# Head 0 of an attention and gated-product kernel: loads and splits in smaller pieces on two queues, the last maxima ranked later, 28 filler products in place of 72

## The chip, the cores and the metric

The kernel runs on one core of a Trainium2 chip. The metric is the device time of one execution in microseconds (us). The core has four compute engines: TensorE (PE in the profile; its weight loads are PEld), VectorE (DVE), ScalarE (ACT) and GpSimd (POOL). SyncE (SP) and ScalarE also issue the DMA transfers.

## The reference

Attention over 4 batches and 8 heads, with q pooled over pairs of rows, and then a gated product over the result:

```python
q_pool = q.reshape(B, H, S // 2, 2, D).mean(axis=3)      # 576 rows a head, D = 64
scores = scale * np.matmul(q_pool, k.transpose(0, 1, 3, 2))   # 576 x 1152
scores = scores - np.max(scores, axis=-1, keepdims=True)
attn = np.exp(scores); attn = attn / (np.sum(attn, axis=-1, keepdims=True) + 1e-09)
x = np.matmul(attn, v)                                   # then (2304, 512)
gate = 1.0 / (1.0 + np.exp(-(x @ w_gate)))               # d_ff = 1536
return (gate * (x @ w_val)) @ w_out
```

## The kernel before

**A head.** There are 32 heads (`u` = 0 to 31). Each fp32 operand is split into a part that TensorE's fp32r format holds and the rest of it. `q_sum` adds the two pooled rows, `q_hi` (ScalarE) rounds, `q_lo` subtracts for the rest; `k_hi` and `k_lo` do the same for K. Then come the *maxima*: for each tile `t` of 128 query rows (five tiles, the last of 64 rows) three products of 384 keys (`mm`, L412 for head 0, L504 for the others), each followed by a row maximum on VectorE (`rmax`, L417 and L510). `all_max` (L329) joins three maxima, and `diags` (L335, L338) writes them as diagonal blocks beside q, so that a score comes out with its maximum already taken off. Only then can the *scores* run (L610: two products for 288 queries by 128 keys, 18 such scores a head in two halves), then the exponentials on ScalarE (L614), then the products with V (L628 in the first batch, 36 instructions a head). The first half (`GR[0]`, queries 0 to 287) waits for the diagonals of tiles 0 to 2 (`got`), the second half for those of tiles 3 and 4 as well (`got1`).

**Head 0** has its own function, `first_head`. Its transfers are cut in pieces (`QS`, `KS`) and its maxima in two groups of tiles (`TS`). Head 1 and the later ones go through `head_operands`: `q_sum` L455 and `q_lo` L465 on GpSimd, `q_hi` L460 and `k_hi` L475 on ScalarE, `k_lo` L481 on GpSimd, `diags` L335 and L338 on GpSimd. The raw q and K lie in one buffer each (`qr`, `kr`). So head 1's q can be loaded (L442) only when head 0's `q_hi`, `q_hi2` and `q_lo` have read `qr`, and head 1's K (L439) only when head 0's `k_hi` and `k_lo` have read `kr`.

**The order.** Nothing runs in the order in which it stands. Every operation goes into a plan, `pl.op(engine, duration, function, priority, after=..., late=...)`. The planner walks through time with these assumed durations: whenever an engine is free, it takes the ready operation with the lowest priority number (an engine other than PE may also hold back for up to `WAIT` = 0.4 us for a more urgent one). `late` is the assumed delay of a transfer after its issue, `behind` puts an issue behind another one. Then 30 rounds of a random search shift some priorities by up to 1 and keep what ends earlier in the plan. The result is one fixed sequence for each engine; on the chip, each engine runs its own sequence in order, and waits at an instruction whose operands are not there.

**The fillers.** `busy` (L951) issues products of a constant tile `sel` with itself into a bank that nothing reads. Before, there are 18 operations of four such products, with priorities from -5.

Of the kernel before, what the change touches and what calls it, by code (L numbers as in the profile page):

```python
# [13 lines left out]
ACTF = mybir.ActivationFunctionType  # L14
ALU = mybir.AluOpType
# [176 lines left out]
def attention_glu_kernel(ctx: ExitStack, tc: tile.TileContext, qT, kT, vt_in, v, wg, wv, wo, out):  # L192
    nc = tc.nc
    B, H, D = 4, 8, 64
    SK, SQ = 1152, 576
# [13 lines left out]
    pl = Plan(SLOTS, ("b",))  # L209
# [6 lines left out]
    late = ctx.enter_context(ExitStack())  # L216
# [96 lines left out]
    AHEAD = 50  # L313
    BUSY = 18
    KEEP = 0.15
    LAST_GATE = 215
    QLP = lambda u: 1 <= u < 2 * H
# [6 lines left out]
    LO, HI, ALL = slice(0, 64), slice(64, 128), slice(0, 128)  # L324


    def all_max(o, ts):
        for p, a, b in ((ALL, ts[0], min(ts[-1] + 1, 4)),) + (((LO, 4, 5),) if 4 in ts else ()):
            nc.vector.tensor_reduce(out=o[p, a:b, 3], in_=o[p, a:b, 0:3], axis=AXX, op=ALU.max, negate=True)  # L329

    def diags(eng, o, q, ts):
        a, b = ts[0], min(ts[-1] + 1, 4)
        q2 = q[1][LO, 128 * a:128 * b].rearrange("p (a c) -> p a c", c=64)
        for par, p in enumerate((LO, HI)):
            eng.tensor_tensor(out=q2[:, par:2 * (b - a):2], in0=ident[p, p].unsqueeze(1).to_broadcast([64, b - a, 64]),  # L335
                              in1=o[p, a:b, 3].unsqueeze(2).to_broadcast([64, b - a, 64]), op=ALU.mult)
        if 4 in ts:
            eng.tensor_tensor(out=q[1][LO, 512:SQ], in0=ident[LO, LO], in1=o[LO, 4, 3:4].to_broadcast([64, 64]), op=ALU.mult)  # L338

    def first_head():  # L340
        kh, qh, kr, qr, pm, vr = (pl.hold(x) for x in ("K", "Q", "kr", "qr", "pm", "ve"))
        QS, KS, TS = ((0, 384), (384, SQ)), ((0, SQ), (SQ, SK)), ((0, 1, 2), (3, 4))
        lq, lk = [], []
        for k, (a, b) in enumerate(QS):

            def load_q(a=a, b=b):
                nc.sync.dma_start(out=tl(qr)[:, :, a:b], in_=qT[0][:, :, a:b])

# [12 lines left out]
        def load_v():
            nc.sync.dma_start(out=tl(vr)[:, :, 0], in_=v[0])

        lv = pl.op("SP", dma(288), load_v, -50, take=[vr], late=3.0)
        lks, qh_done, max_in, kb = (lk[:2], lk[2:]), [], [], []
        for k, (a, b) in enumerate(QS):

            def q_sum(a=a, b=b):
                r = tl(qr)
                nc.vector.tensor_tensor(out=r[:, 0, a:b], in0=r[:, 0, a:b], in1=r[:, 1, a:b], op=ALU.add)  # L370

            def q_hi(a=a, b=b):
                nc.scalar.activation(out=tl(qh)[0][LO, a:b], in_=tl(qr)[:, 0, a:b], func=ACTF.Copy)

            def q_lo(a=a, b=b):
                qa = tl(qh)[0]
                eng = nc.gpsimd if a else nc.vector
                eng.tensor_tensor(out=qa[HI, a:b], in0=tl(qr)[:, 0, a:b], in1=qa[LO, a:b].bitcast(F32),
                                  op=ALU.subtract)

            o = pl.op("DVE", dve(b - a), q_sum, -40 + 4 * k, after=[lq[k]], uses=[qr])
            o = pl.op("ACT", act(b - a), q_hi, -40 + 4 * k, after=[o], uses=[qr] + ([qh] if k else []), take=[] if k else [qh])
            qh_done.append(o)
            max_in.append(pl.op("POOL" if k else "DVE", 0.6 if k else 0.5, q_lo, -40 + 4 * k, after=[o], uses=[qr, qh]))
        ka = []
        for k, (a, b) in enumerate(KS):

            def k_hi(a=a, b=b):
                nc.scalar.activation(out=tl(kh)[0][:, a:b], in_=tl(kr)[:, a:b], func=ACTF.Copy)

            def k_lo(a=a, b=b):
                nc.gpsimd.tensor_tensor(out=tl(kh)[1][HI, a:b], in0=tl(kr)[HI, a:b], in1=tl(kh)[0][HI, a:b].bitcast(F32),
                                        op=ALU.subtract)

            o = pl.op("ACT", act(SQ), k_hi, -39 + 2 * k, after=lks[k], uses=[kr] + ([kh] if k else []),
                      take=[] if k else [kh])
            ka.append(o)
            kb.append(pl.op("POOL", pool(SQ), k_lo, -12 + k, after=[o, max_in[1]], uses=[kr, kh]))

        def q_hi2():  # L400
            nc.scalar.activation(out=tl(qh)[1][HI, 0:SQ], in_=tl(qr)[:, 0], func=ACTF.Copy)

        qb = pl.op("ACT", act(SQ), q_hi2, -35, after=qh_done, uses=[qr, qh])
        dg = []
        for k, ts in enumerate(TS):
            red = []
            for t in ts:
                for j in range(3):
                    m = pl.hold("b")

                    def mm(t=t, j=j, m=m):
                        nc.tensor.matmul(out=tl(m)[LO if t == 4 else ALL, 0:384], lhsT=tl(qh)[0][:, t * 128:min(SQ, t * 128 + 128)],  # L412
                                         rhs=tl(kh)[0][:, j * 384:(j + 1) * 384], start=True, stop=True)

                    def rmax(t=t, j=j, m=m):
                        p = LO if t == 4 else ALL
                        nc.vector.tensor_reduce(out=tl(pm)[p, t, j:j + 1], in_=tl(m)[p, 0:384], axis=AXX, op=ALU.max)  # L417

                    new = not (k or red)
                    a = pl.op("PE", pe(384), mm, -21 + 3 * t + j, after=[max_in[k]] + ([ka[0]] if j == 0 else ka),  # L420
                              uses=[qh, kh], take=[m])
                    red.append(pl.op("DVE", 0.49, rmax, -21 + 3 * t + j, after=[a], uses=[m] + ([] if new else [pm]),
                                     take=[pm] if new else [], keep=KEEP))

            o = pl.op("DVE", 0.1, lambda ts=ts: all_max(tl(pm), ts), -21 + 3 * ts[-1] + 2.5, after=red, uses=[pm])
            dg.append(pl.op("DVE", 1.0 if len(ts) > 2 else 0.7, lambda ts=ts: diags(nc.vector, tl(pm), tl(qh), ts),
                            -21 + 3 * ts[-1] + 2.6, after=[o], uses=[pm, qh]))
        return dict(k=kh, q=qh, v=vr, lv=lv, got=[dg[0], qb] + max_in + ka + kb, dg1=[dg[1]], hi_k=ka, hi_q=qh_done + [qb])

    def head_operands(u, need):  # L430
        if u == 0:
            return first_head()
# [524 lines left out]
    xs, x_done = {}, {}
    blocked = [pl.hold(tag) for tag, n in LATE.items() for _ in range(n)]
# [79 lines left out]
```

## Time and profile before

| | us |
|---|---|
| median of 3 timed runs | 920.72 (920.59 to 921.58) |
| span of the profiled execution, first to last instruction | 919.1 |
| median less that span | 1.6 |
| PE busy in the profile | 910.0 |
| head 0's first filler, first maximum product, first score | 2.73, 9.58, 16.65 |

The profile comes from one execution. A group's busy time over its count is the time of one instruction. The products on PE overlap, so that the distance between starts is what one more product costs. The granted clock stands at 1.00 in all 40 slices of the span.

### The profile page before, as it was taken

The page shows a single profiled execution, that of the slowest core. Times are in us where ns is not written, and L with a number is a line of the kernel's source. Part 1 is how long each engine was busy: PE and PEld are TensorE (multiplying, and loading weights), DVE is VectorE, ACT ScalarE, POOL GpSimd, SP SyncE. Part 2 cuts the span into 40 slices and gives each one's busy share as a digit, 9 for nine tenths or more (in the row PEclk, how much of TensorE's full clock was granted, in tenths as well). Part 3 has the DMA queues.
Part 4 walks back from the last instruction along what each step waited for, and adds up shares of the span by engine and source line. Part 5 has one row for each costly group of instructions (what it writes and reads, how often), then busy time and mean ns, then how long its engine had stood idle before and what let it go on. Part 6 is the DMA issues. An engine that isn't in the chain of part 4 may idle for free.

```text
span 919.1 us, 18605 instructions
## 1 busy us (share of the span) xinstructions
PE 910.0 (99%) x6371; PEld 882.8 (96%) x6371; DVE 649.5 (71%) x1427; ACT 657.5 (72%) x1703; POOL 671.1 (73%) x669
## 2 busy tenths in 40 slices
PE   8999999999999999999999999999999999999998
PEld 8888888999999999999999999999999999999998
DVE  6677779888898987878787878877777874510112
ACT  4798899989998886777887677677877767422111
POOL 6765366889888989889899888888889877521211
PEclk9999999999999999999999999999999999999999
DMA  6899888788868666555644455554545423435432
GB/s 140 212 289 247 275 254 261 239 266 273 262 210 275 206 202 192 161 157 149 166 136 142 131 157 157 160 148 132 166 123 158 142 93 115 166 139 183 162 115 75
DMA packets 57616, 166.27 MB, mean 181 GB/s; under 512 B 17393, under 2 KB 21745, under 8 KB 51377
## 3 DMA queue, kind: packets, MB, share of 16 engines
q1 hardware_dynamic: 57360, 164.78, 59.3%
q8 instruction: 50, 0.82, 0.4%
q10 hardware_dynamic: 160, 0.30, 0.1%
q14 instruction: 46, 0.37, 0.1%
HBM read 132.12 MB, written 23.59 MB: 169 GB/s over the span
## 4 chain that ended last, share of the span: by engine, by line
PE 91%; ACT 4%; DVE 3%; POOL 1%; DMA 1%; issue 1%; POOLq 0%; ACTq 0%; DVEq 0%
PE bank L846 47%; PE bank L610 15%; PE bank L504 7%; PE bank L628 7%; PE bank L657 6%; PE bank L653 6%; PE bank L730 1%; DVE pm L417 1%; PE bank L951 1%; DMA wg<-wg_d 1%; ACT eh L614 1%; ACT bank L643 0%; ACT KA L475 0%; DMA wo<-wo_d 0%; DVE el L646 0%
## 5 line engine op out<-in xcount | busy, mean ns | idle before, releaser
L846 PE MATMUL bank<-x,wg 128*128 128x288 f32 x2304 | 353.8, 295 | 0.0
L846 PEld LDWEIGHTS bank<-x,wg 128*128 128x128 f32 x2304 | 325.6, 188 | 1.1 <-ACT sg L889 0.4
L646 DVE TENSOR_TENSOR el<-bank,eh 128x288 fp32r<-128x288 f32 x432 | 192.9, 452 | 70.7 <-ACT bank L643 65.9
L510 DVE TENSOR_REDUCE pm<-bank 128x1 f32<-128x384 f32 (+1 forms) x375 | 199.7, 550 | 49.6 <-PE bank L504 45.0
L614 ACT ACTIVATE eh<-bank 128x288 fp32r<-128x288 f32 x432 | 176.4, 409 | 73.1 <-PE bank L610 65.9
L643 ACT ACTIVATE bank<-bank 128x288 f32<-128x288 f32 x432 | 176.9, 410 | 0.2
L610 PE MATMUL bank<-QA,KA 128*128 128x288 f32 x576 | 175.1, 308 | 1.5 <-DVE pm L510 0.9
L610 PE MATMUL bank<-QB,KB 128*128 128x288 f32 x576 | 167.4, 295 | 0.0
L903 POOL TENSOR_TENSOR g<-sg,g 128x288 fp32r<-128x288 f32 x96 | 79.9, 833 | 105.2 <-ACT g L899 102.7
L675 POOL TENSOR_TENSOR acc<-acc,eh 128x576 f32<-128x576 f32 x92 | 132.5, 1440 | 16.7 <-ACT eh L614 14.6
L846 PE MATMUL bank<-g,wo 128*128 128x288 f32 x864 | 139.2, 295 | 0.2
L657 PE MATMUL bank<-el,vt 128*128 128x288 f32 x432 | 127.2, 296 | 0.5 <-DVE el L646 0.5
L653 PE MATMUL bank<-eh,vt 128*128 128x288 f32 x432 | 127.3, 296 | 0.0
L846 PEld LDWEIGHTS bank<-g,wo 128*128 128x128 f32 x864 | 125.0, 188 | 1.2 <-DMA wo<-wo_d 0.3
L504 PE MATMUL bank<-KA,QA 128*128 128x384 f32 (+1 forms) x375 | 125.7, 350 | 0.2
L610 PEld LDWEIGHTS bank<-QA,KA 128*128 128x128 f32 x576 | 108.2, 188 | 5.9 <-DVE pm L510 1.3
L610 PEld LDWEIGHTS bank<-QB,KB 128*128 128x128 f32 x576 | 108.3, 188 | 1.3
L895 DVE SCALAR_TENSOR_TENSOR sg<-sg,bank 128x288 f32<-128x288 f32 x96 | 43.3, 451 | 81.2 <-PE bank L846 79.2
L657 PEld LDWEIGHTS bank<-el,vt 128*128 128x128 f32 x432 | 81.1, 188 | 1.5 <-DVE el L646 1.2
L653 PEld LDWEIGHTS bank<-eh,vt 128*128 128x128 f32 x432 | 81.1, 188 | 0.7 <-ACT eh L614 0.3
L675 POOL TENSOR_TENSOR acc<-eh,eh 128x576 f32<-128x576 f32 x48 | 68.7, 1431 | 15.6 <-ACT eh L614 10.9
L628 PE MATMUL bank<-e,ve 128*128 128x288 f32 x288 | 76.6, 407 | 0.0
(86 smaller groups left out, 1359.6 us busy)
## 6 DMA issues: line engine op xcount, KB each, us to landing
wg<-wg_d SPq DMA_DIRECT2D x48, 1024.0 KB, 5.2
wo<-wo_d SPq DMA_DIRECT2D x36, 512.0 KB, 3.9
kr<-in_kT_dram SPq DMA_DIRECT2D x62, 288.0 KB, 5.0
wg_d<-cs SPq DMA_DIRECT2D x24, 512.0 KB, 5.0
qr<-in_qT_dram SPq DMA_DIRECT2D x31, 288.0 KB, 4.1
KP<-KA SPq DMA_DIRECT2D x30, 288.0 KB, 4.4
vr<-in_v_dram SPq DMA_DIRECT2D x24, 288.0 KB, 3.1
cr<-in_wg_dram SPq DMA_DIRECT2D x12, 512.0 KB, 5.3
```

Source lines behind the costliest of these rows:

```text
L504: nc.tensor.matmul(out=tl(m)[LO if t == 4 else ALL, 0:384], lhsT=lhs(t), rhs=rhs()[:, j * 384:(j + 1) * 384], start=True, stop=True)
L510: nc.vector.tensor_reduce(out=o, in_=tl(m)[p, 0:384], axis=AXX, op=ALU.max)
L610: nc.tensor.matmul(out=tl(m)[:, 0:GN], lhsT=tl(hd["k"])[k][:, ks], rhs=tl(hd["q"])[k][:, a:b], start=(k == 0), stop=(k == 1))
L614: nc.scalar.activation(out=ev(), in_=tl(m)[:, 0:GN], func=ACTF.Exp, scale=1.0 / 16.0)
L628: nc.tensor.matmul(out=tl(av[0])[:, 0:GN], lhsT=pair(c, 0), rhs=tl(h), start=(c == 0), stop=(c == NC - 1))
L643: nc.scalar.activation(out=p, in_=p, func=ACTF.Exp, scale=1.0 / 16.0)
L646: nc.vector.tensor_tensor(out=tl(el), in0=tl(m)[:, 0:GN], in1=ev().bitcast(F32), op=ALU.subtract)
L653: nc.tensor.matmul(out=tl(av[0])[:, 0:GN], lhsT=pair(c, w), rhs=ev(), start=(c == 0), stop=(c == NC - 1))
L657: nc.tensor.matmul(out=tl(av[1])[:, 0:GN], lhsT=pair(c, 1 - w), rhs=tl(el), start=(c == 0), stop=(c == NC - 1 and not mine_c))
L675: nc.gpsimd.tensor_tensor(out=tl(acc), in0=tl(old).bitcast(F32), in1=tl(eh).bitcast(F32), op=ALU.add)
L846: nc.tensor.matmul(out=ps[:, 0:GN], lhsT=l, rhs=r, start=(n == 0 and j == 0), stop=(n == 3 and j == 2))
L903: nc.gpsimd.tensor_tensor(out=g[:, 1, a:b], in0=tl(sg), in1=g[:, 0, a:b].bitcast(F32), op=ALU.subtract)
```

## The change

It touches head 0 and the fillers, and nothing else in the text of the kernel; the order of everything is planned anew.

- q is loaded in three pieces (128, 256 and 192 columns) and K in three (384 each, two halves of 64 partitions), where there were two of each. The second piece of q goes on ScalarE's queue, as the first of K does already.
- The first two pieces of q are summed and split on VectorE; the third is summed and split on GpSimd, with low priorities. `k_lo` has three pieces. `q_hi2` has two.
- A maximum product waits only for the pieces that it reads. The maxima, `all_max` and `diags` of tiles 3 and 4 get priorities from -1 on, where they had -12 on. The first half of the scores no longer waits for the third piece of q.
- The fillers are 14 operations of two products, with priority 999.

```diff
-    BUSY = 18
+    BUSY = 14
...
-        QS, KS, TS = ((0, 384), (384, SQ)), ((0, SQ), (SQ, SK)), ((0, 1, 2), (3, 4))
+        QS, KS, TS = ((0, 128), (128, 384), (384, SQ)), ((0, 384), (384, 768), (768, SK)), ((0, 1, 2), (3, 4))
...
+            def load_q(a=a, b=b, eng=nc.scalar if k == 1 else nc.sync):
+                eng.dma_start(out=tl(qr)[:, :, a:b], in_=qT[0][:, :, a:b])
+
+            lq.append(pl.op("ACT" if k == 1 else "SP", 0.6, load_q, (-60, -55, -53)[k], uses=[qr] if k else [], take=[] if k else [qr], late=(1.7, 2.2, 3.4)[k],
...
+                lk.append(pl.op("SP" if k else "ACT", 0.6, load_k, (-59, -57, -57)[k], uses=[] if new else [kr],
+                                take=[kr] if new else [], late=(2.0, 2.2, 3.0)[k], behind=lk[0] if k == 1 and not n else lk[-1] if lk else None))
...
-        lks, qh_done, max_in, kb = (lk[:2], lk[2:]), [], [], []
+        lks, qh_done, max_in, kb = (lk[:2], lk[2:4], lk[4:]), [], [], []
...
+                (nc.gpsimd if a > 128 else nc.vector).tensor_tensor(out=r[:, 0, a:b], in0=r[:, 0, a:b], in1=r[:, 1, a:b], op=ALU.add)
...
+            o = pl.op("POOL" if a > 128 else "DVE", pool(b - a) if a > 128 else dve(b - a), q_sum, (-40, -36, -18.5)[k], after=[lq[k]], uses=[qr])
...
+            max_in.append(pl.op("POOL" if a > 128 else "DVE", pool(b - a) if a > 128 else dve(b - a), q_lo, (-40, -36, -11)[k], after=[o], uses=[qr, qh]))
...
-            kb.append(pl.op("POOL", pool(SQ), k_lo, -12 + k, after=[o, max_in[1]], uses=[kr, kh]))
...
+            kb.append(pl.op("POOL", pool(b - a), k_lo, -20 + k, after=[o, max_in[1]], uses=[kr, kh]))
...
+            qb.append(pl.op("ACT", act(b - a), q_hi2, -30 if a else -35, after=qh_done[2 * (a > 0):2 + (a > 0)], uses=[qr, qh]))
...
-                    a = pl.op("PE", pe(384), mm, -21 + 3 * t + j, after=[max_in[k]] + ([ka[0]] if j == 0 else ka),
...
+                    a = pl.op("PE", pe(384), mm, (-10 if k else -21) + 3 * t + j, after=[max_in[2 if k else min(t, 1)]] + ka[:j + 1],
...
-        return dict(k=kh, q=qh, v=vr, lv=lv, got=[dg[0], qb] + max_in + ka + kb, dg1=[dg[1]], hi_k=ka, hi_q=qh_done + [qb])
+                            (-10 if k else -21) + 3 * ts[-1] + 2.6, after=[o], uses=[pm, qh]))
+        return dict(k=kh, q=qh, v=vr, lv=lv, got=[dg[0], qb[0]] + max_in[:2] + ka + kb, dg1=[dg[1], qb[1], max_in[2]], hi_k=ka, hi_q=qh_done + qb)
...
-            for _ in range(4):
+            for _ in range(2):
...
-            pl.op("PE", 0.7 if k < 6 else 0.36, busy, -5 + 0.01 * k, uses=[bz] if k else [], take=[] if k else [bz])
+            pl.op("PE", 1.5 if k == 0 else 0.44, busy, 999 + 0.01 * k, uses=[bz] if k else [], take=[] if k else [bz])
```

## Rows read from the trace of the kernel before

**Rows 1.** The page's 40 slices: TensorE's busy share and granted clock, in tenths.

```profile
PE   8999999999999999999999999999999999999998
...
PEclk9999999999999999999999999999999999999999
```

**Rows 2.** Stretches: length, busy (count) of PE, PEld, DVE, ACT, POOL, clock, DMA.

```profile
2.73:9.58 6.85, 6.85 (x32) 6.85 (x33) 1.55 (x5) 2.82 (x6) 5.50 (x7) 1.00 1.15 238
...
16.65:32.37 15.72, 15.67 (x84) 13.38 (x83) 9.67 (x26) 11.70 (x28) 10.50 (x10) 1.00 0.50 142
32.37:915.90 883.53, 880.38 (x6203) 855.56 (x6202) 629.58 (x1373) 640.91 (x1668) 649.52 (x642) 1.00 0.60 182
```

**Rows 3.** Timeline of TensorE: start, length, what; 16.65 begins the scores.

```profile
2.73 7.01 PE L951 MATMUL bank<-sel 128*128 128x192 f32 x32 [2.73 <-DVE sel L991]
9.58 0.72 PE L412 MATMUL bank<-KA,QA 128*128 128x384 f32 x3
10.14 0.58 PE L951 MATMUL bank<-sel 128*128 128x192 f32 x4
10.56 1.25 PE L412 MATMUL bank<-KA,QA 128*128 128x384 f32 x6
...
14.88 1.93 PE L951 MATMUL bank<-sel 128*128 128x192 f32 x16
16.65 0.31 PE L610 MATMUL bank<-QA,KA 128*128 128x288 f32 x1
...
20.73 1.49 PE L504 MATMUL bank<-KA,QA 128*128 128x384 f32 x4
```

**Rows 4.** Timeline of VectorE: start, length, what, idle time before it.

```profile
4.68 0.55 DVE L370 TENSOR_TENSOR qr<-qr 64x384 f32<-64x384 f32 x1 [1.85 <-DMA qr<-in_qT_dram]
...
9.98 4.32 DVE L417 TENSOR_REDUCE pm<-bank 128x1 f32<-128x384 f32 x9 [3.37 <-PE bank L412]
14.34 0.16 DVE L329 TENSOR_REDUCE pm<-pm 128x3 f32<-128x9 f32 x1
...
15.26 2.87 DVE L417 TENSOR_REDUCE pm<-bank 128x1 f32<-128x384 f32 x6
```

**Rows 5.** Timeline of ScalarE: head 0's first exponentials, head 1's splits.

```profile
17.13 1.45 ACT L614 ACTIVATE e<-bank 128x288 f32<-128x288 f32 x4 [6.12 <-PE bank L610]
18.48 0.67 ACT L460 ACTIVATE QA<-qr 64x576 fp32r<-64x576 f32 x1
...
19.87 1.26 ACT L475 ACTIVATE KA<-kr 128x576 fp32r<-128x576 f32 x2
```

**Rows 6.** Timeline of GpSimd: the constants, then head 1's operands and diagonals.

```profile
3.44 2.05 POOL L996 MEMSET KB<- 64x1152 f32 x2
...
12.54 1.41 POOL L455 TENSOR_TENSOR qr<-qr 64x576 f32<-64x576 f32 x1
19.22 1.42 POOL L465 TENSOR_TENSOR QA<-qr,QA 64x576 fp32r<-64x576 f32 x1 [5.27 <-ACT QA L460]
20.71 2.78 POOL L481 TENSOR_TENSOR KB<-kr,KA 64x576 fp32r<-64x576 f32 x2
...
30.04 1.29 POOL L335 TENSOR_TENSOR QB<-ident,pm 64x256 fp32r<-64x256 f32 x2
31.41 0.28 POOL L338 TENSOR_TENSOR QB<-ident,pm 64x64 fp32r<-64x64 f32 x1
```

**Rows 7.** DMA issues of the first 2.2 us: KB each, median us to landing.

```profile
kr<-in_kT_dram ACTq DMA_DIRECT2D x2, 144.0 KB, 3.5
qr<-in_qT_dram SPq DMA_DIRECT2D x1, 192.0 KB, 3.9
```

**Rows 8.** Timeline of TensorE: head 1's first score.

```profile
32.37 0.29 PE L610 MATMUL bank<-QA,KA 128*128 128x288 f32 x1
```

**Rows 9.** The chain that ended last, by time: a run of scores, products with V.

```profile
28.12 0.53 PE bank L610 x4
...
33.41 1.46 PE bank L628 x6
```

More of the change, by code (lines that the diff above doesn't have):

```diff
@@ L341, in first_head @@
         kh, qh, kr, qr, pm, vr = (pl.hold(x) for x in ("K", "Q", "kr", "qr", "pm", "ve"))
-        QS, KS, TS = ((0, 384), (384, SQ)), ((0, SQ), (SQ, SK)), ((0, 1, 2), (3, 4))
+        QS, KS, TS = ((0, 128), (128, 384), (384, SQ)), ((0, 384), (384, 768), (768, SK)), ((0, 1, 2), (3, 4))
         lq, lk = [], []
         for k, (a, b) in enumerate(QS):
-            def load_q(a=a, b=b):
-                nc.sync.dma_start(out=tl(qr)[:, :, a:b], in_=qT[0][:, :, a:b])
-            lq.append(pl.op("SP", 0.6, load_q, -60 + 2 * k, uses=[qr] if k else [], take=[] if k else [qr], late=2.4,
+            def load_q(a=a, b=b, eng=nc.scalar if k == 1 else nc.sync):
+                eng.dma_start(out=tl(qr)[:, :, a:b], in_=qT[0][:, :, a:b])
+            lq.append(pl.op("ACT" if k == 1 else "SP", 0.6, load_q, (-60, -55, -53)[k], uses=[qr] if k else [], take=[] if k else [qr], late=(1.7, 2.2, 3.4)[k],
                             behind=lq[-1] if lq else None))
@@ L356, in load_k @@
                     eng.dma_start(out=tl(kr)[p, a:b], in_=kT[0][:, a:b])
-                lk.append(pl.op("SP" if k else "ACT", 0.6, load_k, -59 + 2 * k, uses=[] if new else [kr],
-                                take=[kr] if new else [], late=2.6, behind=lk[-1] if lk else None))
+                lk.append(pl.op("SP" if k else "ACT", 0.6, load_k, (-59, -57, -57)[k], uses=[] if new else [kr],
+                                take=[kr] if new else [], late=(2.0, 2.2, 3.0)[k], behind=lk[0] if k == 1 and not n else lk[-1] if lk else None))
         def load_v():
@@ L369, in q_sum @@
                 r = tl(qr)
-                nc.vector.tensor_tensor(out=r[:, 0, a:b], in0=r[:, 0, a:b], in1=r[:, 1, a:b], op=ALU.add)
+                (nc.gpsimd if a > 128 else nc.vector).tensor_tensor(out=r[:, 0, a:b], in0=r[:, 0, a:b], in1=r[:, 1, a:b], op=ALU.add)
             def q_hi(a=a, b=b):
@@ L376, in q_lo @@
                 qa = tl(qh)[0]
-                eng = nc.gpsimd if a else nc.vector
+                eng = nc.gpsimd if a > 128 else nc.vector
                 eng.tensor_tensor(out=qa[HI, a:b], in0=tl(qr)[:, 0, a:b], in1=qa[LO, a:b].bitcast(F32),
                                   op=ALU.subtract)
-            o = pl.op("DVE", dve(b - a), q_sum, -40 + 4 * k, after=[lq[k]], uses=[qr])
+            o = pl.op("POOL" if a > 128 else "DVE", pool(b - a) if a > 128 else dve(b - a), q_sum, (-40, -36, -18.5)[k], after=[lq[k]], uses=[qr])
             o = pl.op("ACT", act(b - a), q_hi, -40 + 4 * k, after=[o], uses=[qr] + ([qh] if k else []), take=[] if k else [qh])
             qh_done.append(o)
-            max_in.append(pl.op("POOL" if k else "DVE", 0.6 if k else 0.5, q_lo, -40 + 4 * k, after=[o], uses=[qr, qh]))
+            max_in.append(pl.op("POOL" if a > 128 else "DVE", pool(b - a) if a > 128 else dve(b - a), q_lo, (-40, -36, -11)[k], after=[o], uses=[qr, qh]))
         ka = []
@@ L393, in k_lo, with q_hi2 @@
                                         op=ALU.subtract)
-            o = pl.op("ACT", act(SQ), k_hi, -39 + 2 * k, after=lks[k], uses=[kr] + ([kh] if k else []),
+            o = pl.op("ACT", act(b - a), k_hi, -39 + 2 * k, after=lks[k], uses=[kr] + ([kh] if k else []),
                       take=[] if k else [kh])
             ka.append(o)
-            kb.append(pl.op("POOL", pool(SQ), k_lo, -12 + k, after=[o, max_in[1]], uses=[kr, kh]))
-        def q_hi2():
-            nc.scalar.activation(out=tl(qh)[1][HI, 0:SQ], in_=tl(qr)[:, 0], func=ACTF.Copy)
-        qb = pl.op("ACT", act(SQ), q_hi2, -35, after=qh_done, uses=[qr, qh])
+            kb.append(pl.op("POOL", pool(b - a), k_lo, -20 + k, after=[o, max_in[1]], uses=[kr, kh]))
+        qb = []
+        for a, b in ((0, 384), (384, SQ)):
+            def q_hi2(a=a, b=b):
+                nc.scalar.activation(out=tl(qh)[1][HI, a:b], in_=tl(qr)[:, 0, a:b], func=ACTF.Copy)
+            qb.append(pl.op("ACT", act(b - a), q_hi2, -30 if a else -35, after=qh_done[2 * (a > 0):2 + (a > 0)], uses=[qr, qh]))
         dg = []
@@ L419, in first_head @@
                     new = not (k or red)
-                    a = pl.op("PE", pe(384), mm, -21 + 3 * t + j, after=[max_in[k]] + ([ka[0]] if j == 0 else ka),
+                    a = pl.op("PE", pe(384), mm, (-10 if k else -21) + 3 * t + j, after=[max_in[2 if k else min(t, 1)]] + ka[:j + 1],
                               uses=[qh, kh], take=[m])
-                    red.append(pl.op("DVE", 0.49, rmax, -21 + 3 * t + j, after=[a], uses=[m] + ([] if new else [pm]),
+                    red.append(pl.op("DVE", 0.49, rmax, (-10 if k else -21) + 3 * t + j, after=[a], uses=[m] + ([] if new else [pm]),
                                      take=[pm] if new else [], keep=KEEP))
-            o = pl.op("DVE", 0.1, lambda ts=ts: all_max(tl(pm), ts), -21 + 3 * ts[-1] + 2.5, after=red, uses=[pm])
+            o = pl.op("DVE", 0.1, lambda ts=ts: all_max(tl(pm), ts), (-10 if k else -21) + 3 * ts[-1] + 2.5, after=red, uses=[pm])
             dg.append(pl.op("DVE", 1.0 if len(ts) > 2 else 0.7, lambda ts=ts: diags(nc.vector, tl(pm), tl(qh), ts),
-                            -21 + 3 * ts[-1] + 2.6, after=[o], uses=[pm, qh]))
-        return dict(k=kh, q=qh, v=vr, lv=lv, got=[dg[0], qb] + max_in + ka + kb, dg1=[dg[1]], hi_k=ka, hi_q=qh_done + [qb])
+                            (-10 if k else -21) + 3 * ts[-1] + 2.6, after=[o], uses=[pm, qh]))
+        return dict(k=kh, q=qh, v=vr, lv=lv, got=[dg[0], qb[0]] + max_in[:2] + ka + kb, dg1=[dg[1], qb[1], max_in[2]], hi_k=ka, hi_q=qh_done + qb)
     def head_operands(u, need):
```

## Prediction

> **What bounds the kernel now.** I read the page's slices first, then the busy time by stretch, then the timelines of the first 35 us engine by engine, because the change touches only head 0, whose work lies there. TensorE is busy in nearly all of every slice after the first [rows 1]. From the first score at 16.65 to the last product at 915.90 it lacks 0.05 + 3.15 = 3.2 us of 899 [rows 2]. So once the scores run, TensorE alone sets the end, and what the change can bring is TensorE's work being done earlier at the start, if TensorE does not wait later instead.
>
> Where do the 16.65 us go? The first sum of q runs at 4.68 [rows 4], so head 0's data are there early. But 32 fillers stand first in TensorE's sequence, from 2.73 to 9.58 [rows 3]: 6.85 / 32 = 0.214 us each. They hold the first maximum product, whose result VectorE starts to reduce at 9.98. Nine maxima take 4.32 us (0.48 each), joining them and writing the diagonals until the next one starts takes 15.26 - 14.30 = 0.96 [rows 4]. Then sixteen more fillers, from 14.88 to 16.65 [rows 3], hold the first score by about 1.3 us after the diagonals. Fillers thus sit in the way twice.
>
> **The first score after.** The order is not in the trace of before, so I walk through the planner's account by hand; its assumed times serve for the order alone. In it q's first piece is there at 0.6 + 1.7 = 2.3 and split at 3.4, K's first piece is split at 3.9. The fillers rank last but nothing else is ready before 3.9: 1.5 + 6 x 0.44 = 4.14, so seven operations, 14 products, still come ahead of the first maximum product. One more operation comes before the second product, and two before tile 1, whose q is split at 5.6 in the account; after that one, and three at the end while TensorE has nothing to do. None stands between the diagonals and the scores.
>
> On the chip: 2.73 + 14 x 0.214 = 5.73 for the first maximum product. Are its data there? Transfers of 144 and 192 KB landed 3.5 and 3.9 us after their issue [rows 7]. A first piece of 64 KB, issued at the same 0.75, should land between 3.0 us (below the shorter of these) and 3.9, so at 3.8 to 4.7. Sum, rounding and subtraction of 128 columns, at no more than the 0.55 of 384 columns [rows 4] and by proportion about 0.3 each, give 4.7 to 5.6. I take that the fillers and not the data set 5.73; the smaller pieces are then hidden by the fillers, and if the cover fails (a landing 0.2 us past the bound) the first product moves by the excess.
>
> The second maximum product stands behind two more fillers, the third behind four more. With a maximum product at twice its later cost while the fillers are still slow (0.35; later at most 1.25 / 6 = 0.21 [rows 3]) tile 1 starts at 5.73 + 0.35 + 0.43 + 0.35 + 0.86 = 7.7. Its reduction starts some 0.5 later (0.40 was seen [rows 3, 4]), at 8.25. Seven reductions remain: 7 x 0.48 = 3.4, to 11.6, then 0.96 for the diagonals and a hand-over: first score at 12.65. Bounds: 11.7 if q's second piece and TensorE let tile 1 run 0.9 earlier; 13.2 if they are 0.6 late. GpSimd is clear: its constants end at 5.49 [rows 6], then three pieces of `k_lo` at 2/3 of 1.39, and the sum and the rest of q's last piece, 192 of 576 columns, at some 0.6 each (576 take 1.41) end near 9.7, before the score at 12.65. The gain there is 16.65 - 12.65 = 4.0.
>
> The maxima of tiles 3 and 4 cost at most 6 x 0.21 = 1.25 on TensorE behind the first score. But the last piece of q is split near 9.7, while TensorE waits for the diagonals; in the account four of the six run in that gap. Two remain: 0.35 to 0.42. So 3.65, if nothing later is late.
>
> **A rule weighed.** The fillers were 0.214 apart up to 9.4, and the four from 10.14 to 10.56 were 0.105 apart [rows 3]: a factor of two, though the granted clock reads 1.00 throughout [rows 1]. The Trainium skill, page "TensorE: Matmul & The Clock Gate", Part 1, says that the array's default is the slow level of 1.2 GHz and that only sustained activity lifts it to 2.4 GHz. The factor in the rows agrees with it, the granted-clock column does not show it. By that rule fewer fillers are no pure saving: with a lift that comes late the time would be rival 3's 921.6, with one as early as in the rows the 918.3 below. My sum takes the higher pace from near 9.4 on as before, since TensorE is occupied without a break from 2.73 to about 10 in both kernels.
>
> **What is late next: head 1.** Its score started at 32.37 [rows 8], 15.72 us after head 0's, and TensorE was busy for 15.67 of that [rows 2]. Its diagonals ended at 31.69 [rows 6], so its chain had only 0.7 to spare. If the scores start 4 us earlier and this chain doesn't, TensorE waits for head 1. So I follow the chain.
>
> Before, q's raw buffer came free first. Now q's last rest is ranked behind all of `k_lo` on GpSimd, so K's buffer comes free first (9.6 against 10.2 in the account), and SyncE loads K ahead of q. In the account K is split and ready for `k_lo` at 15.52, and q lands at 15.93: 0.41 later, and GpSimd holds back only for 0.4. So it takes half of `k_lo`, then `q_sum`, the other half, and `q_lo`. ScalarE's sequence becomes six exponentials, K's splits, six exponentials, then `q_hi`. (That 0.01 decides here is why the other order is a rival.)
>
> With durations from rows: the first exponential runs 0.48 after the first score and each takes 0.36 [rows 3, 5]: 13.13 + 6 x 0.36 = 15.3; K's split 0.63 [rows 5], 16.0 with the hand-over; half of `k_lo` 1.39, `q_sum` 1.41 [rows 6], 18.8. On TensorE six scores (6 x 2 x 0.133), two groups of products with V (2 x 1.46 [rows 9]) and two maxima put the seventh score at 17.5, so the seventh exponential at 18.0 and the twelfth's end at 20.15. Then `q_hi` 0.67 and `q_lo` 1.42 [rows 5, 6]: 22.3. Head 1's maxima thus start at 22.3 where they started at 20.73 [rows 3]: later, though everything before is earlier.
>
> From there 0.4 + 15 x 0.48 to 29.9, 0.2 for the join (0.16 for three tiles [rows 4]), then the diagonals, 31.69 - 30.04 = 1.65 [rows 6], to 31.8: head 1's first score at 31.9. Before it was 32.37, with one group of products with V (1.46) still to do for head 0. After, head 0 is finished, and TensorE may fill its wait with up to 1.2 us of head 2's maxima. The lead is 0.47 + 1.46 = 1.9 without these, up to 3.1 with them, less the 0.2 of head 2 that had run before 32.37: 1.7 to 2.9. I take 2.4, nearer to the upper end because those maxima have nothing else to wait for. After that TensorE sets the pace again and keeps the lead.
>
> **The sum.** 919.1 - 2.4 = 916.7 for the span; the median lies 1.6 above the span, so 918.3. Of 3.65 gained at the start, 1.25 is lost again waiting for head 1.
>
> **Rivals.** (1) *Head 1 is not late.* A random shift in the search flips the 0.01, GpSimd sums q first, `q_lo` ends near 17.5, and TensorE never waits: lead 3.65, 917.1. For it: the margin; against: few of the 30 rounds fall on this stretch. (2) *Given back in the order.* The whole sequence is planned anew. TensorE's 3.2 us of waits after 16.65 [rows 2] can become half as much again or more, and head 1 may be later than 22.3 by the 1.4 of another `k_lo` half: lead 0 to 1.5, about 920.0. (3) *Slower.* The slow spacing lasts past the first score, because from 5.73 on only 14 short fillers and waiting maxima occupy TensorE, and no fillers stand in the last gap. The slow stretch before lasted 9.4 - 2.73 = 6.7 us; a second one over scores and products would lose half of it, 3.3: -2.4 + 3.3 = +0.9, 921.6. It turns the sign when it lasts more than 4.8 us in real work; once more during the wait for head 1 would make it some 924. For it: fillers are what fell away. Against: in the trace the pace, once up, never fell.
>
> **The numbers.** A measurement tells a difference of 0.2% (1.8 us) from none: faster is below 918.9, slower above 922.6. The forecast has 0.43, with a range of its own from 917.3 (a first score 0.95 earlier) to 919.6 (0.6 later, and no maxima of head 2 in the wait): 0.30 of it is faster, 0.13 the same. Rival 1 has 0.22, all faster. Rival 2 has 0.20: 0.16 the same, 0.04 slower if the waits more than double. Rival 3 has 0.15: 0.05 the same (one slow stretch), 0.10 slower (a longer one, or two). So faster 0.52, same 0.34, slower 0.14. The range leaves out rival 1 with an early first score (917.1 - 0.6 = 916.5) and most of rival 3, above 921.2.
>
> **What would show it.** First maximum product at 5.7, first score at 11.7 to 13.2 with no fillers behind the diagonals; head 1's K loaded ahead of its q; `q_lo` L465 at about 20.9; a wait of TensorE before head 1's first score at about 31.9. Filler starts 0.214 apart and scores 0.133 apart (four in 0.53 [rows 9]) show the pace; scores at 0.27 apart would make rival 3 true. The forecast is wrong if head 1's maxima start before 19 or after 25.

## The result and the profile after

The kernel after takes 930.43 us (median of 4, 930.30 to 930.68), before 920.65 (920.53 to 921.58): a ratio of 1.0106, 95% interval 1.0094 to 1.0118. It is 1% slower; 918.3 was forecast. The span of the profiled execution is 928.5, 9.4 more than before. PE is busy for 909.7 us of it (910.0 before), although 44 fillers fewer run.

TensorE's timeline after (start, length, what, idle time before it and what ended it; L415 are head 0's maxima, L613 the scores, L507 the later heads' maxima, L954 the fillers):

```profile
2.73 3.30 PE L954 MATMUL bank<-sel 128*128 128x192 f32 x14 [2.73 <-DVE sel L994]
5.83 0.57 PE L415 MATMUL bank<-KA,QA 128*128 128x384 f32 x1
...
11.59 0.29 PE L613 MATMUL bank<-QA,KA 128*128 128x288 f32 x1
14.20 0.40 PE L613 MATMUL bank<-QB,KB 128*128 128x288 f32 x1 [2.31 <-DVE QB L335]
...
21.76 0.40 PE L613 MATMUL bank<-QB,KB 128*128 128x288 f32 x1 [1.68 <-DVE QB L338]
...
27.05 1.55 PE L507 MATMUL bank<-KA,QA 128*128 128x384 f32 x8
...
34.99 2.16 PE L507 MATMUL bank<-KA,QA 128*128 128x384 f32 x8 [2.26 <-POOL QA L468]
37.02 0.61 PE L613 MATMUL bank<-QA,KA 128*128 128x288 f32 x1
```

The first maximum product came 3.75 us earlier than in [rows 3]. The product of the first score that reads the diagonals ran at 14.20 (before 16.80), the second half of the scores stopped until 21.76, and head 1's first score ran at 37.02 instead of 32.37 [rows 8]. VectorE's timeline after shows what both stops waited for:

```profile
7.03 1.05 DVE L378 TENSOR_TENSOR QA<-qr,QA 64x256 fp32r<-64x256 f32 x1
...
12.24 0.16 DVE L329 TENSOR_REDUCE pm<-pm 128x3 f32<-128x9 f32 x1
12.51 1.63 DVE L335 TENSOR_TENSOR QB<-ident,pm 64x192 fp32r<-64x192 f32 x2
14.06 2.40 DVE L420 TENSOR_REDUCE pm<-bank 128x1 f32<-128x384 f32 x5
...
18.59 1.66 DVE L335 TENSOR_TENSOR QB<-ident,pm 64x64 fp32r<-64x64 f32 x2
20.28 1.43 DVE L338 TENSOR_TENSOR QB<-ident,pm 64x64 fp32r<-64x64 f32 x1
27.42 7.05 DVE L513 TENSOR_REDUCE pm<-bank 128x1 f32<-128x384 f32 x15 [5.71 <-PE bank L507]
```

Before, the diagonals and the first score product that reads them stood like this:

```profile
14.61 0.72 DVE L335 TENSOR_TENSOR QB<-ident,pm 64x192 fp32r<-64x192 f32 x2
16.80 0.30 PE L610 MATMUL bank<-QB,KB 128*128 128x288 f32 x1
18.34 0.45 DVE L335 TENSOR_TENSOR QB<-ident,pm 64x64 fp32r<-64x64 f32 x2
18.82 0.22 DVE L338 TENSOR_TENSOR QB<-ident,pm 64x64 fp32r<-64x64 f32 x1
```

The second group of diagonals, three products of 64 by 64, took 0.45 + 0.22 before and 1.66 + 1.43 after. GpSimd's timeline after, in the same stretch:

```profile
5.56 2.24 POOL L392 TENSOR_TENSOR KB<-kr,KA 64x384 fp32r<-64x384 f32 x2
...
12.17 1.40 POOL L575 TENSOR_TENSOR vt<-vr,vt 128x576 fp32r<-128x576 f32 x1 [1.90 <-ACT vt L571]
17.25 1.41 POOL L484 TENSOR_TENSOR KB<-kr,KA 64x576 fp32r<-64x576 f32 x1 [3.69 <-ACT KA L478]
18.74 1.42 POOL L458 TENSOR_TENSOR qr<-qr 64x576 f32<-64x576 f32 x1
20.23 1.40 POOL L484 TENSOR_TENSOR KB<-kr,KA 64x576 fp32r<-64x576 f32 x1
24.48 1.41 POOL L468 TENSOR_TENSOR QA<-qr,QA 64x576 fp32r<-64x576 f32 x1 [2.85 <-ACT QA L463]
```

Each VectorE product that was long ended within 0.3 us after a GpSimd product that ran beside it: the rest of q's second piece (L378) at 8.08 and GpSimd's at 7.80, the first of the first group at 13.77 and 13.57 (the second then took 0.35), the last two of the second group at 20.25 and 20.16 and at 21.71 and 21.63. In [rows 6] GpSimd stood idle from 13.95 to 19.22, while VectorE wrote the diagonals.

Then TensorE's pace. Stretches of 1 us after (length, PE busy with its products, granted clock, DMA):

```profile
36.00:37.00 1.00, 0.97 (x4) 0.83 0.51 96
37.00:38.00 1.00, 1.00 (x5) 0.50 0.89 267
38.00:39.00 1.00, 0.98 (x4) 0.50 1.07 218
39.00:40.00 1.00, 1.00 (x6) 0.50 0.94 181
40.00:41.00 1.00, 1.00 (x6) 0.96 0.97 324
```

After the 2.3 us of idle time before 34.99 and eight maxima 0.25 us apart, the granted clock was 0.50, the 1.2 GHz level, from about 36.7 to 40.1, and scores started 0.24 us apart instead of 0.133.

**How far behind it is, and where.** To compare two kernels in the middle I sum the products that TensorE still has to do, each at its usual spacing (scores and gated products 0.133 us, maxima 0.173, products with V in the first batch 0.243, fillers 0; 886.0 us in all). A kernel is behind by the time by which it has the same sum left later than before. The kernel after, in us:

| at | 16 | 20 | 32 | 36 | 40 | 44 | 130 | 270 | 330 | end |
|---|---|---|---|---|---|---|---|---|---|---|
| behind | -2.6 | -2.9 | -1.2 | 1.7 | 3.6 | 3.7 | 5.6 | 8.7 | 9.1 | 9.4 |

So it led by 2.6 us, lost 6.3 between 16 and 44 us, and 5.7 more afterwards, in a part whose text the change leaves alone. In the view of waits, the longest that end a stop of TensorE after 44 us are (who waited for whom; total us, times, longest):

```profile
PE bank L613 <- DVE el L649: 1.8, 3, 0.8
PE bank L613 <- ACT e L617: 1.0, 2, 0.8
PE bank L660 <- DVE el L649: 0.9, 1, 0.9
PE bank L849 <- DMA wo<-wo_d: 0.7, 1, 0.7
```

They are spread over many places; before, the same view shows 0.9, 0.7 and 0.5 and nothing else. All that the view lists adds up to 5.8 us after and 2.1 before, so these stops cover 3.7 of the 5.7. The order of the whole kernel is another one.

### The profile page after: what moved, and what is told of

It is laid out like the page before. It is cut to its first block, busy times and chain, and to the rows that moved or that the text cites. A ratio compares the mean times of both kernels' runs of the same rounds, so it can differ in the third digit from the quotient of the medians.

```text
span 928.5 us, 18549 instructions
## 1 busy us (share of the span) xinstructions
PE 909.7 (98%) x6327; PEld 878.1 (95%) x6327; DVE 654.5 (70%) x1428; ACT 660.8 (71%) x1706; POOL 671.5 (72%) x671
## 4 chain that ended last, share of the span: by engine, by line
PE 91%; DVE 3%; ACT 3%; issue 1%; POOL 1%; DMA 1%; DVEq 0%; ACTq 0%; POOLq 0%
PE bank L849 47%; PE bank L613 16%; PE bank L507 7%; PE bank L631 7%; PE bank L660 6%; PE bank L656 6%; PE bank L733 1%; DVE pm L513 1%; DMA wo<-wo_d 1%; DVE pm L420 0%; ACT KA L478 0%; ACT eh L617 0%; ACT bank L646 0%; PE bank L954 0%; DVE QB L335 0%
## 5 line engine op out<-in xcount | busy, mean ns | idle before, releaser
L613 PE MATMUL bank<-QA,KA 128*128 128x288 f32 x576 | 177.8, 312 | 3.6 <-DVE el L649 1.8
L613 PE MATMUL bank<-QB,KB 128*128 128x288 f32 x576 | 168.4, 296 | 4.0 <-DVE QB L335 2.3
L507 PE MATMUL bank<-KA,QA 128*128 128x384 f32 x375 | 123.1, 347 | 2.4 <-POOL QA L468 2.3
L613 PEld LDWEIGHTS bank<-QA,KA 128*128 128x128 f32 x576 | 108.9, 189 | 10.5 <-DVE el L649 2.6
L613 PEld LDWEIGHTS bank<-QB,KB 128*128 128x128 f32 x576 | 109.1, 189 | 6.0 <-DVE QB L335 2.6
L892 ACT ACTIVATE sg<-bank 128x288 f32<-128x288 f32 x96 | 39.4, 411 | 57.2 <-PE bank L849 54.7
L678 POOL TENSOR_TENSOR acc<-eh,eh 128x576 f32<-128x576 f32 x48 | 68.7, 1432 | 14.8 <-ACT eh L617 12.5
```

Source lines behind the costliest of these rows:

```text
L613: nc.tensor.matmul(out=tl(m)[:, 0:GN], lhsT=tl(hd["k"])[k][:, ks], rhs=tl(hd["q"])[k][:, a:b], start=(k == 0), stop=(k == 1))
L678: nc.gpsimd.tensor_tensor(out=tl(acc), in0=tl(old).bitcast(F32), in1=tl(eh).bitcast(F32), op=ALU.add)
```

## The experiments

Sixteen kernels (the numbers are names; there is no 10). "At 44" and "later" are the lag against the profile of before at 44 us, and what was added to it by the end, worked out as above. They come from one execution of each kernel, and executions of one kernel differ: the profiled one of run 15 took 934.34, the slowest of its three, that of run 14 926.66, 1.6 above its median, and that of run 5 922.07, 1.2 above.

| kernel | median us | ratio to before (95%) | at 44 | later |
|---|---|---|---|---|
| after | 930.43 | 1.0106 (1.0094 to 1.0118) | 3.7 | 5.7 |
| 1 before, no search | 926.14 | 1.0060 (1.0043 to 1.0077) | -0.7 | 5.6 |
| 2 after, no search | 928.01 | 1.0086 (1.0062 to 1.0110) | 1.3 | 5.1 |
| 3 before, few fillers, same order | 919.41 | 0.9988 (0.9978 to 0.9997) | -1.4 | -0.1 |
| 4 after, diagonals on ScalarE, same order | 928.92 | 1.0094 (1.0076 to 1.0111) | 1.4 | 5.8 |
| 5 before with the new fillers alone | 920.91 | 1.0003 (0.9994 to 1.0012) | -0.2 | 1.2 |
| 6 before, seed 2 | 926.24 | 1.0056 (1.0041 to 1.0071) | -0.2 | 5.5 |
| 7 as 3, diagonals on GpSimd | 918.09 | 0.9974 (0.9965 to 0.9984) | -3.4 | 0.1 |
| 8 after, fillers in the wait, same order | 928.82 | 1.0088 (1.0073 to 1.0103) | 1.3 | 6.0 |
| 9 after, 400 rounds | 929.80 | 1.0100 (1.0082 to 1.0118) | 1.5 | 7.6 |
| 11 before, GpSimd busy, same order | 920.57 | 1.0002 (0.9992 to 1.0012) | -1.1 | 0.1 |
| 12 after, head 1's q first | 930.37 | 1.0096 (1.0077 to 1.0115) | -0.8 | 10.4 |
| 13 after, diagonals on GpSimd, same order | 928.35 | 1.0083 (1.0070 to 1.0097) | 1.8 | 6.3 |
| 14 before, seed 3 | 925.06 | 1.0048 (1.0032 to 1.0065) | -0.7 | 6.5 |
| 15 after, seed 3 | 930.61 | 1.0115 (1.0090 to 1.0141) | 6.0 | 7.4 |
| 16 after, seed 4 | 928.37 | 1.0082 (1.0065 to 1.0099) | 1.1 | 5.9 |
| 17 as 7, priorities of 300 rounds | 924.77 | 1.0041 (1.0027 to 1.0055) | -3.4 | 7.9 |

**1 and 2: no random search.**

```diff
-    order = pl.search(30, 30.0, 1.0)
+    order = pl.search(0, 30.0, 1.0)
```

> The kernel before, its order written without the 30 rounds of random search. Theory A (part of the loss is that the search found less for the new plan than for the old one): in the planner's own account the search shortens the plan of before by 4.2 and that of after by 0.8, so without it before should take about 920.7 + 4.2 = 924.9, at least 922.5. Theory B (all of the loss comes from head 0 and head 1, the order of the rest makes no difference on the chip): 919.7 to 921.7.

> The kernel after without the random search. Theory A: 930.4 + 0.8 = 931.2, so that the difference to before without search is about 6 instead of 9.8. Theory B: 930.4, a difference of 9.8 as with search.

Before lost 5.2 us without the search, all of it after 44 us: the order there is worth that much, and theory B fell. After took 2.4 us less without it, where the planner's account had said a loss of 0.8; its four executions went from 926.77 to 931.56. Without search the two kernels are 1.9 us apart instead of 9.8.

**3: before's own order, fewer fillers.**

```diff
-            for _ in range(4):
+            for _ in range(n):
...
-            pl.op("PE", 0.7 if k < 6 else 0.36, busy, -5 + 0.01 * k, uses=[bz] if k else [], take=[] if k else [bz])
+            pl.op("PE", 0.7 if k < 6 else 0.36, lambda k=k: busy(2 if k < 8 else 1), -5 + 0.01 * k, uses=[bz] if k else [], take=[] if k else [bz])
```

> The kernel before in exactly its own order; only each filler operation issues fewer products (two in the first eight, one in the other ten: 26 instead of 72). Theory A (in before the fillers hold the first maximum product by 3.0 us and the first score by 1.3 more, and head 1 follows the exponentials): first maximum product at 6.7, first score near 12.5, all later work 4 us earlier: 916.7. Theory B (fillers are what keeps TensorE at the higher pace; with fewer, the scores run slowly for some us): 919 to 922, with scores 0.27 apart near 13 us.

1.5 us were won, about a third of what theory A had said. 919.41 lies in theory B's range, but without its sign: from 14.25 on the scores started 0.13 us apart. The first maximum product ran at 6.75, and the first score's second product at 14.25 instead of 12.5, because VectorE's diagonals, now 2.3 us earlier, met GpSimd's products:

```profile
12.27 1.83 DVE L335 TENSOR_TENSOR QB<-ident,pm 64x192 fp32r<-64x192 f32 x2
...
17.11 2.62 DVE L335 TENSOR_TENSOR QB<-ident,pm 64x64 fp32r<-64x64 f32 x2
19.76 1.33 DVE L338 TENSOR_TENSOR QB<-ident,pm 64x64 fp32r<-64x64 f32 x1
```

The lead that was there at 44 us stayed to the end within 0.1 us. With the order held, a lead at the start is kept. At 16 us it had been 2.5; by 32 us 1.3 of it were gone, because the second group of diagonals held VectorE, and with it head 1's row maxima, until 21.0.

**4: head 0's diagonals on ScalarE.**

```diff
+                nc.scalar.activation(out=q[1][LO, 128 * t + 64 * par:128 * t + 64 * par + 64], in_=ident[p, p],
+                                     func=ACTF.Copy, scale=o[p, t, 3:4])
...
-            dg.append(pl.op("DVE", 1.0 if len(ts) > 2 else 0.7, lambda ts=ts: diags(nc.vector, tl(pm), tl(qh), ts),
+            dg.append(pl.op("DVE", 1.0 if len(ts) > 2 else 0.7, lambda ts=ts: diags_act(tl(pm), tl(qh), ts),
```

> The kernel after in exactly its own order; only head 0's diagonal products run on ScalarE, as ten small activations with a scale for each partition, in place of VectorE's products of two tensors in SBUF. Theory A (VectorE's products were held by GpSimd's concurrent products, 1.66 and 1.43 us where 0.45 and 0.22 were seen before; the second half of the scores, head 1 and the fall of TensorE's pace follow from it): the scores of the second half start near 19.5 instead of 21.8, head 1's first score near 34.5 instead of 37.0, 926 to 928.5. Theory B (head 1 is late because of its loads and the order on GpSimd alone): head 1's first score within 0.7 of 37.0 and 929.8 to 931.

Inconclusive: 928.92 lies between the two, and head 1's first score at 36.55 is as theory B had it. The edit brings its own cost: the six activations of the first group (there are nine in all) took 2.15 us, more than the 1.63 of the stretched products, and TensorE idled for 2.5 us. The second half went on without a stop, but its slow stretch came at 13.7 to 17.1 here.

**5, 6, 9: one part alone, another seed, a longer search.** Run 5 is the kernel before with the diff's three lines on fillers; run 6 has `random.Random(2)`; run 9 has the priorities that 400 rounds find.

> Of the change, only the fillers: the kernel before with 14 operations of two products, ranked last, planned and searched anew. Theory A (fillers in the way cost before some 4 us at the start, of which 1.5 were kept when their number was cut in the old order; the rest of the order now comes from a new search, whose plan is 0.6 longer): 920.9 - 1.5 + 0.6 = 920.0, between 918.5 and 921.5, with a lead near 40 us that is not kept exactly. Theory B (the fillers are what made the change slow): 925 or more.

> The kernel before with nothing changed but the seed of the random search (2 instead of 1). Theory A (luck of the search moves the end by some us, whatever the kernel): the plan is 3.2 longer, so 924, with the first 40 us as before and the loss growing later. Theory B (the order of the rest is worth nothing on the chip): within 1 us of before.

> The kernel after with the priorities that 400 rounds of the search find instead of 30; its plan is 3.6 shorter. Theory A: the loss by 44 us stays at 2 to 4, the loss after that falls from 5.7 to about 2: 925 to 928. Theory B (the later loss follows from head 0 and head 1 being late, whatever the order): 929.5 to 931.

The fillers alone, with the new order that they bring, are worth nothing in either direction. Nothing but the seed changed before by 5.7 us, more than the difference of the plans (3.2), and after 44 us. Run 9 lies in theory B's range, and the simple form of theory A falls: its plan was 3.6 us shorter, yet the chip lost 7.6 us after 44. But theory B's reason does not hold either. By the same account run 9 lost only 1.1 us from 44 to 330 us, where after lost 5.4, and 6.5 behind 330, where after lost 0.3: so the later loss is not bound to a late head 0 and head 1. How long the plan is doesn't tell how good the order is on the chip.

**8: fillers where TensorE waits.**

```diff
                 def mm(t=t, j=j, m=m):
+                    if at == 2 * HS - 21 and t == j == 0:
+                        for _ in range(20):
+                            nc.tensor.matmul(out=tl(m)[:, 0:192], lhsT=sel[:, 0:2].rearrange("p a d -> p (a d)"),
+                                             rhs=sel.rearrange("p a d -> p (a d)"), start=True, stop=True)
```

> The kernel after in its own order, with 20 more filler products where TensorE waits at 32.7 for head 1's and head 2's operands (2.3 us of idle time). Theory A (the idle time there is what lets TensorE's pace fall to half from 36.7 to 40.1): the pace stays up there, 1.7 us are won, 928 to 929.3. Theory B (the fall has to do with the sparse products of the stretch before, or costs nothing because head 1 waits for VectorE anyway): 929.8 to 931.

As theory A had it, 1.6 us less, and in the profiled execution the granted clock stayed at 1.00 to the last products of the kernel:

```profile
37.00:38.00 1.00, 0.96 (x6) 1.00 1.07 258
38.00:39.00 1.00, 1.00 (x9) 1.00 1.13 205
39.00:40.00 1.00, 1.00 (x7) 1.00 0.88 266
```

Two of the four executions had a mean granted clock of 1.00 (928.15 and 928.45 us), the other two 0.998 (929.18 and 929.73); all four of after had 0.998 or 0.996. That it was the fillers that kept the pace up is not shown: in runs 4 and 12 the same wait, 2.26 and 2.25 us long and without fillers, was not followed by a fall. What the fall costs is clearer: between 32 and 44 us runs 4 and 8, without it, each lost 2.9 us, and after 4.9.

**11: GpSimd busy beside the diagonals of before.**

```diff
+            if u == 1:
+                for _ in range(6):
+                    z = TL["tt"][0]
+                    nc.gpsimd.tensor_tensor(out=z, in0=z, in1=z, op=ALU.add)
```

> The kernel before, with six additional GpSimd sums of a scratch tile with itself (128x288) right after head 1's sum of q, in the time when VectorE writes head 0's diagonals. Theory A (a product of two tensors on VectorE is held while GpSimd works on two tensors): VectorE's diagonal products, 0.35 and 0.22 us each in before, take 0.8 us or more each where they meet GpSimd's sums (0.8 us each), while the row maxima from PSUM beside them stay at 0.48; the total stays within 1.5 us of before, because the fillers stand behind the first diagonals. Theory B (they were long in the kernel after for another reason, such as the write to a tile that others use): 0.35 and 0.22 as in before.

Theory A, in the kernel before and in its own order (the scratch tile is also cleared once at the start). VectorE, then GpSimd:

```profile
13.54 1.33 DVE L335 TENSOR_TENSOR QB<-ident,pm 64x192 fp32r<-64x192 f32 x2
14.80 2.87 DVE L417 TENSOR_REDUCE pm<-bank 128x1 f32<-128x384 f32 x6
17.69 0.21 DVE L329 TENSOR_REDUCE pm<-pm 128x1 f32<-128x3 f32 x2
17.88 2.08 DVE L335 TENSOR_TENSOR QB<-ident,pm 64x64 fp32r<-64x64 f32 x2
19.99 1.46 DVE L338 TENSOR_TENSOR QB<-ident,pm 64x64 fp32r<-64x64 f32 x1
```

```profile
13.88 4.50 POOL L459 TENSOR_TENSOR tt<-tt 128x288 f32<-128x288 f32 x6
18.46 1.42 POOL L469 TENSOR_TENSOR QA<-qr,QA 64x576 fp32r<-64x576 f32 x1
19.95 2.79 POOL L485 TENSOR_TENSOR KB<-kr,KA 64x576 fp32r<-64x576 f32 x2
```

The same products take 1.33, 2.08 and 1.46 us instead of 0.72, 0.45 and 0.22, while the six row maxima beside them, which read PSUM (the banks that TensorE writes), take their 2.87 as in [rows 4]. The added sums took 0.67 us each, and single products beside them 0.57 to 0.73, less than the 0.8 that was expected; the last two met head 1's products of 1.42 us and took 1.49 and 1.46. The Trainium skill, page "GPSIMD Engine Reference", section "Specifications", says that GpSimd shares its interfaces to SBUF with VectorE, with contention for VectorE instructions that have two SBUF inputs. The rows agree, and show how long: such a product was not done until the GpSimd instruction beside it was over. The total is as before, since the fillers stand behind the first diagonals there.

**13 and 12: which of two reasons makes head 1 late.** Run 13 replaces `nc.vector` by `nc.gpsimd` in head 0's `diags`. Run 12 moves three operations in the finished order (`q_ops` are head 1's `q_sum`, `q_hi` and `q_lo`, `k_op` is its first `k_hi`):

```diff
+    q_ops, k_op = moved[:3], moved[3]
+    order = [o for o in order if o not in q_ops]
+    order[order.index(k_op):order.index(k_op)] = q_ops
```

> The kernel after in its own order; head 0's diagonal products run on GpSimd, so that they can't meet a GpSimd product. Theory A (the stretched second diagonals hold the second half's scores, and with them TensorE's whole sequence and head 1's maxima): second half's scores at 19.5 to 20.0 (21.8 in after), head 1's first maximum product at 25.0 to 25.6 (27.05), 927 to 929. Theory B (head 1's operands are late because of GpSimd's order, and here its K is split 2 us later still): head 1's maxima at 27 or later, 930 to 932.

> The kernel after in its own order, but head 1's sum, rounding and rest of q are moved ahead of the split of its K on GpSimd and ScalarE. Theory P (the step of the prediction: GpSimd's half of K ahead of q's sum makes head 1 late): head 1's q is split 4 to 5 us earlier, its maxima start 3 us or more before 27.05, 926 to 928. Theory A (TensorE's own sequence, held by the second half's scores at 21.8, sets the start of head 1's maxima): its q is split 4 us earlier, but the first maximum product stays between 26.3 and 27.7, 929.5 to 931.

Run 13 took 2.1 us less than after, within theory A's range, although head 1's K was split 3 us later. Its two marks were missed: the second half went on at 20.5, half a microsecond past the range, and head 1's maxima began at 26.25 (27.05 in after), 0.65 past it; slow stretches came at 14.6 and 35.1.

In run 12 head 1's q was split 6.9 us earlier, and its maxima came 2.6 us earlier, at 24.44: less than theory P wanted and more than A. GpSimd's new sequence also spared the first group of diagonals and two products of the second, and this alone accounts for the gain. The first score's second product ran 1.30 us earlier, at 12.90, and the stop before the second half was 0.37 instead of 1.68 us, 2.61 in all. From there to head 1's maxima TensorE ran without a stop in both kernels, 19.16 to 24.44 here (5.28 us) and 21.76 to 27.05 in after (5.29). So theory A's reason stands, and the earlier q won nothing at this place. The run was 0.8 us ahead of before at 44 us, and still took 930.37 (one of four executions, with a mean granted clock of 1.00, 926.73): in the profiled one TensorE then waited 2.2 us at 82 us and ran at 0.50 from 86.1 to 89.5.

**7: few fillers, diagonals on GpSimd.** Run 3 with `diags(nc.gpsimd, ...)` for head 0.

> The kernel before in its own order with few fillers (as in the run that took 919.4), and head 0's diagonal products on GpSimd. Theory A (there too VectorE's diagonals, now earlier, met GpSimd's products: 1.83, 2.62 and 1.33 us instead of 0.72, 0.45 and 0.22): first score 0.5 to 0.8 earlier, head 1's row maxima no longer held until 21.0, 1 to 1.5 us won: 918 to 918.6. Theory B (GpSimd is the tighter engine, head 1's rest of q is pushed back by the diagonals): 919 to 921.

Theory A: 2.4 us faster than the executions of before beside it, and the fastest of all. GpSimd's diagonals take 1.09 and 0.92 us, and TensorE waits 0.34 for them where it waited 1.15 in run 3:

```profile
12.42 1.09 POOL L335 TENSOR_TENSOR QB<-ident,pm 64x192 fp32r<-64x192 f32 x2
...
17.58 0.63 POOL L335 TENSOR_TENSOR QB<-ident,pm 64x64 fp32r<-64x64 f32 x2
18.28 0.29 POOL L338 TENSOR_TENSOR QB<-ident,pm 64x64 fp32r<-64x64 f32 x1
```

**14 to 17: is the later loss the draw, or the change?** More seeds, and run 7 with the priorities of a longer search.

> The kernel before with seed 3 of the random search (plan 1.9 longer than with seed 1). Theory A (the order of before is a good draw; a new draw costs some us after 44 us in any kernel): first 44 us as before within 1, then a loss of 1 to 7 us, 922 to 927. Theory B (the kernel before is always good, the loss belongs to the change): 920 to 921.5.

> The kernel after with seed 3 of the random search (plan 0.2 longer than with seed 1). Theory A: 1 to 4 us behind at 44 us, then a loss that differs from 5.7 by up to some us either way: 924 to 932. Theory B: 5.7 again within 0.7, 928 to 930.5.

> The kernel after with seed 4 (plan 0.6 longer than with seed 1). As for seed 3: theory A 924 to 932 with a later loss that differs from seed to seed, theory B 5.7 again within 0.7.

> The fastest version so far (before's fillers cut to 26 products, head 0's diagonals on GpSimd; 918.1) with the priorities that 300 rounds of search find for it; the plan is 1.1 shorter. Theory A (the plan's length says little about the chip, and the 30-round order was a good draw): 919 to 924. Theory B (a shorter plan is faster): 917.0.

Run 14 went as theory A had it, and run 15 by its later loss of 7.4, though in its slowest execution. Run 16's 5.9 is what theory B had named as well, and decides nothing. Run 17 came out 0.8 past theory A's range and far from theory B's 917.0: it has the head 0 and the lead of run 7 and a shorter plan, and lost 7.9. Taken together, new orders of the kernel before lost 5.5, 5.6 and 6.5 us after 44; orders of after 5.1, 5.7, 5.9, 7.4 and 7.6. With before's order held, the three kernels that differ at the start (3, 7 and 11) differ by 0.1 from then on. Run 5 shows that a new draw can be nearly as good (1.2).

## Why the prediction was wrong

- **First maximum product: right.** 5.73 was forecast, 5.83 measured; 14 fillers, then 2, then 4, and none behind the diagonals. The smaller pieces of the loads were hidden as said, up to this product. K loaded ahead of head 1's q, GpSimd's order of half of K, q, half of K, rest of q, and ScalarE's six exponentials before K's split: all as walked through.
- **Tile 1 and the reductions: 0.6 late, at the bound.** The rest of q's second piece took VectorE 1.05 us beside GpSimd's `k_lo`, where the sum of the same 256 columns had taken 0.42. Tile 1 started at 8.13 instead of 7.7 and the reductions ended at 12.2 instead of 11.6.
- **The term for the diagonals: mis-sized.** "0.96 for the diagonals" came from a stretch in which GpSimd stood idle. Moving the diagonals earlier put them beside GpSimd's products; the first group took 1.63 instead of 0.72, and the first score that needs it ran at 14.20, past the bound of 13.2: from the end of the reductions to this score it was 2.0 us. The second group took 3.1 us instead of 0.7, and the forecast has no stop there: by its seventh score at 17.5 the second half would have begun near 18.3, and it stopped until 21.76. Run 11 shows the cause by itself.
- **Head 1's chain: its order was right, the wait that ends last was not.** Its rest of q began at 24.48 where about 20.9 was forecast, because the exponentials ahead of its rounding wait for the second half's scores. The forecast let this rest of q set the start of head 1's maxima, at 22.3. It ended at 25.89, but TensorE, held up by the second half's diagonals, reached the maxima only at 27.05, past the 25 that was named as a sign of being wrong. Head 1's first score came at 37.02 instead of 31.9.
- **The wait for head 1: longer than priced.** Head 2's maxima were to fill it, as they "have nothing else to wait for". They waited 2.26 us for head 2's rest of q. Every profile of a kernel with the change has this stop of 2.3 us, whatever its order, but for run 8, whose fillers stand in it; so it belongs to the change and not to the draw.
- **Rival 3 came in part.** The slow pace did not last past the first score, but came back at 36.7, after the wait that the forecast had named as its second place. Run 8, whose profile is without it, took 1.6 us less.
- **The step that failed most: "After that TensorE sets the pace again and keeps the lead."** The lag grew by 5.7 us after 44 us. It was priced as rival 2, at 0 to 1.5 us of lead left, with the waits of before taken as typical. They were not: three new orders of the unchanged kernel lost 5.5 to 6.5 us there. The change forced a new order, and this alone cost about as much as everything at the start.
- **The sum as measured**: -2.6 at 16 us, 6.3 lost by 44 (most of it: 1.7 in the stop for the second diagonals, 2.3 in the wait for heads 1 and 2, about 2 in the slow pace), 5.7 from the later order: 9.4.

Open: why one order is better than another by 5 us after 44 us. The stops are many and under a microsecond, and no run took them apart. What makes the pace fall after one wait and not after another of the same length is open too.

## What to carry to other kernels

When an order is searched and the best one kept, the kernel at hand can be a good draw; an edit that makes the planner draw again can lose that (nine of ten new orders here lost 5 to 8 us after 44, one 1.2), so test an edit with the order held, and count the new draw as a cost of its own. A duration read from a row holds for the neighbours that the row had: for an operation that moves, look at what the other engines do at its new time. Fillers can be cut in place: run 3 gets 1.5 us from it without a new plan, and run 7, with the diagonals moved out of GpSimd's way as well, 2.4.

## What the runs showed of the hardware

A VectorE product with two inputs in SBUF stood until the GpSimd product beside it ended, 1.43 us for one that takes 0.22; row maxima from PSUM beside GpSimd's sums of run 11 kept their 0.48. A short idle time was followed by a loss of TensorE's pace in some runs and not in others: in after, behind 2.3 us of idle time and eight maxima 0.25 us apart, the granted clock was 0.50 for some 3 us; in runs 4 and 12 it stayed at 1.00 after the same wait, and in the profile of run 8, with 20 fillers in that wait, too.
